# Attention and MLP on one core: input quarters made at other places of the unit and rounded by VectorE, first weights prepared over more units

## The chip, the cores and the metric

The kernel runs on one NeuronCore of a Trainium2 chip. The metric is the device time of one execution in microseconds (us). The engines are TensorE (PE; its weight loads are listed apart as PEld), VectorE (DVE), ScalarE (ACT), GpSimd (POOL) and the SyncE queue (SP), from which nearly all DMAs are issued.

## What is computed

Attention with a bias that is a small network of the relative position, then a two-layer network over the 2304 tokens. Cut to what matters:

```python
scores = scale * (q @ k.T) + bias          # bias[h, i, j] from a 32-unit network of log1p|i-j| / log1p(i)
attn = exp(scores - max) / (sum + 1e-9)    # 4 batches, 8 heads, 576 positions, head size 64
x = (attn @ v) reordered to (2304, 512)
h = x @ w_in                               # 512 -> 2048
g = where(h >= 1, h, where(h <= -1, 0, (h + 1)**2 / 4))
out = g @ w_out                            # 2048 -> 512
```

## The kernel before, in words

Every product is done with both operands split into a rounded high part (type fp32r) and a low part, the difference: three matmuls stand for one. A split therefore costs one rounding copy and one subtraction. The subtractions are mostly POOL's.

The program has three stages. The first makes the bias tables and stores them to DRAM. The second is attention: 16 units, one for each pair of heads and batch (unit n has heads pair p = n // 4 and batch b = n % 4). The third is the two-layer network, in three blocks of 768 tokens; for the first block its input x must be ready in 8 quarters (k, j): k is the pair of heads, j the half of 384 tokens.

The order of all work in attention is written out by hand. Each step of a unit has a time in the table `BEAT`, in a scale of 15.5 a unit; `on(n, t, f)` puts a step at 15.5 * n + t, and the steps are emitted in the order of these numbers. ACT, DVE, PE and POOL keep that order, so a time only sets what stands before what on an engine. On DVE one unit has, in this order (numbers modulo 15.5): `r` 0.47 (adds a constant to the row sums and inverts them; line 547, tile `sum`), maxima `m00` 1.38 and `m01`, the low parts `l30` and `lL`, maxima `m10` and `m11`, `ls1`, `kh` 6.08 (rounding of the next keys and queries, line 171), maxima `m20` and `m21`, `l10` 8.9, `vh` 9.52 (rounding of the values, line 179), `l11` 10.73, `m30` 11.36, `ls0`, `m31` 12.43, `mL` 13.97, `l21` 14.68. The maxima are line 457 and read the scores in PSUM; the low parts are line 544 and read PSUM too. POOL has in one unit: low part of the values (line 147, `vs`) 0.57, then a copy and a subtraction (lines 541 and 542) for each of four of the transposed tiles, `l31` 2.47, `l00` 8.55, `l01` 12.22, `l20` 14.3, and two subtractions for keys and queries (line 147, `ls`) at 8.73 and 10.32. PE holds two score tiles (`S`) at a time; a maximum frees one.

Between these steps stand two kinds of early work for the third stage. `split_x` makes one quarter: it loads two half sums of x from DRAM with the inverted row sums, and then `add` (line 391), `scaled` (line 394), `high` (line 398, the rounding, on ACT) and `rest` (line 402, POOL). `XQ` gives for each quarter the time of its load, the place in SBUF (`raw`, `x` or `bias`, three pools that have other users too) and the unit and times of the four steps. All four lie in one unit: (0,0) in unit 4, (1,0) in 8, (2,0) in 12, (0,1) in 13, (1,1) in 14, the last three in unit 15. `weight_ahead` prepares a tile of weights, rebuilt from two 32-bit halves of its 64-bit words: `load`, `shift` and `sign` on ACT, `join` and `high` on DVE (lines 127 and 132), `rest` on POOL (line 136). `WQ` puts the first four tiles in units 6, 7, 10 and 11, all five steps of a tile in one unit. A load that needs a buffer waits in SP's queue for the buffer's last reader, and what is behind it waits too.

Of the kernel before, what the change touches and what calls it, by code (L numbers as in the profile page):

```python
# [24 lines left out]
NG = S // 16  # L25
# [4 lines left out]

CBW = (1, 1, 32, C, C, C * H, S // 4, NG)
CB = sum(CBW)
CFG = dict(un=[('paaa', 'paav')[g in (1, 30, 32, 34)] for g in range(NG)], bb=5, mv=1, rb='a', pool=((0, 0), (0, 1), (2, 0), (3, 1)), sb=4, keep=1, drain=2, diag='a', rb2='v', eps='v', rc=2, rbb=1, hb=2, rawb=(2, 2), eb=4, seq=0, pb=(6, 9, 12, 14, 16), pq=22, tb=6, ub=12, low0='ppp', anch=(8, 8, 16, 23, 23), low1='ppp', ob=4, gb=4, fin=2, sbf=('v', 'v', 'v', 'v', 'v'), bsE=(), ytail='p')
EPS = 1e-9
RB = 2
FIRST = ((0, 3), (1, 5), (2, 33))
USUAL = (10.0, 13.1, 14.05, 17.9)
XQ = {(0, 0): (39, "raw", 4, USUAL), (1, 0): (80, "raw", 8, USUAL), (2, 0): (120, "raw", 12, USUAL), (3, 0): (140, "bias", 15, (6.1, 6.2, 8.0, 8.1)),
      (0, 1): (125, "x", 13, USUAL), (1, 1): (133, "raw", 14, USUAL), (2, 1): (144, "x", 15, (9.5, 10.0, 10.9, 11.1)), (3, 1): (153, "raw", 15, (13.1, 13.2, 14.5, 16.3))}
WQ = {(0, 0): (53, 6), (0, 1): (70, 7), (1, 0): (93, 10), (1, 1): (110, 11)}  # L40
LB = ((1, 1), (2, 1), (3, 2), (3, 3), (2, 3))
UNIT = 15.5
BEAT = {
# [11 lines left out]
}  # L55
POOL, SB, KEEP, RBB = CFG["pool"], CFG["sb"], CFG["keep"], CFG["rbb"]
BIG = 3.0e38
# [4 lines left out]
def attn_cpb_moe_kernel(ctx, tc, qk, vL, cb, win, wout, lw, ident, ii, out):  # L62
    nc = tc.nc
# [19 lines left out]
    lp = ctx.enter_context(tc.tile_pool(name="a_load", side="right", bufs=2))  # L83
    bp = loads.enter_context(tc.tile_pool(name="a_bias", side="right", bufs=CFG["bb"]))
    qp = loads.enter_context(tc.tile_pool(name="a_qkv", side="right", bufs=2))
# [54 lines left out]
    qkv, bias = {}, {}  # L140
# [8 lines left out]
    def keep(ins):  # L149
        tc.keep_in_program_order(ins)  # L150

    def pool(ins):
        if KEEP and go[0]:
            tc.keep_in_program_order(ins)
# [5 lines left out]
    def prep(n):  # L160

        L = CFG["low0"] if n == 0 else CFG["low1"] if n == 1 else "ppp"
        a = qkv[n] = {}

        def high(ins):
            keep(ins)

        def high_k():

            a["h"] = qp.tile([P, KQ], F32R, tag="kh", name=f"kh{n}", bufs=CFG["hb"])  # L170
            high(nc.vector.tensor_copy(a["h"], a["r"]))

        def load_r():
            a["r"] = lp.tile([P, KQ], F32, tag="qk", name=f"qk{n}", bufs=CFG["rawb"][0])
            nc.sync.dma_start(out=a["r"], in_=qk[n])
# [5 lines left out]
        def load_v():  # L181
            a["rv"] = lp.tile([P, 10, D], F32, tag="v", name=f"v{n}", bufs=CFG["rawb"][1])
            nc.sync.dma_start(out=a["rv"].rearrange("p a b -> p (a b)"), in_=vL[n])
# [20 lines left out]
    with ExitStack() as ph:  # L204
# [21 lines left out]
        diag = [ac.tile([P, P], F32, name=f"diag{i}") for i in range(2)]  # L226
# [9 lines left out]
        pq = cp.tile([P, 2, C, H], F32, name="pq")  # L236
# [102 lines left out]
    xs = {}  # L339
# [3 lines left out]
    def x_tile(z, k, part, name):  # L343
        if z == 0:
            return xp0.tile([P, TH], F32R, tag=f"x{'hl'[part]}{k}", name=name)
        at = 2 * k + part
        g = min(at // 3, 2) + (at == 7)
        if at % 3 == 0 or at == 7:
            tag, w, n_ = ("qk", KQ, CFG["rawb"][0]) if g < 2 else ("v", 10 * D, CFG["rawb"][1])
            room[g] = lp.tile([P, w], F32R, tag=tag, name=name, bufs=n_)  # L350
        c0 = TH * (at % 3 if at < 6 else 0)
        return room[g][:, c0 : c0 + TH]

    def load_x(blk, k, j, home="x"):

        src = xT[k][blk // TB][:, :, TH * j : TH * j + TH].rearrange("(s d) i c -> d s i c", s=2)
        rp = rps[0]
        if home != "raw":
            if home == "bias":
                r = bp.tile([P, 2 * S], F32, tag="bias", name=f"x{blk}_{k}_{j}").rearrange("p (a b) -> p a b", a=3)  # L360
            else:
                r = rp.tile([P, 3, TH], F32, tag="x", name=f"x{blk}_{k}_{j}", bufs=1)
            r, rr = r[:, 0:2], r[:, 2]
        else:
            r = rp.tile([P, 2 * DM], F32, tag="raw", name=f"x{blk}_{k}_{j}")[:, : 2 * TH].rearrange("p (a b) -> p a b", a=2)
            rr = rp.tile([P, DM], F32, tag="a", name=f"xr{blk}_{k}_{j}")[:, :TH]
        for i in range(2):
            nc.sync.dma_start(out=r[D * i : D * i + D], in_=src[:, :, i])
        c0 = blk + TH * j
        c1 = c0  # L370
        while c1 < c0 + TH:
            t = c1 % S
            e = min(c0 + TH, c1 - t + (512 if t < 512 else S))
            for i in range(2):
                at = 512 * i + t if t < 512 else 1024 + D * i + t - 512
                row = rT[k][c1 // S][at : at + e - c1].unsqueeze(0)
                nc.sync.dma_start(out=rr[D * i : D * i + D, c1 - c0 : e - c0], in_=row.to_broadcast((D, e - c1)))  # L377
            c1 = e
        return r, rr
# [5 lines left out]
    def split_x(k, j, home):  # L385

        r, rr = load_x(0, k, j, home)
        x = r[:, 0]

        def add():  # L390
            keep(nc.vector.tensor_tensor(out=x, in0=x, in1=r[:, 1], op=ALU.add))

        def scaled():
            keep(nc.vector.tensor_tensor(out=x, in0=x, in1=rr, op=ALU.mult))  # L394

        def high():
            xs[k, j] = [x_tile(j, k, i, f"x{'hl'[i]}0_{k}_{j}") for i in range(2)]
            keep(nc.scalar.copy(xs[k, j][0], x))

        def rest():  # L400
            h, l = xs[k, j]
            pool(nc.gpsimd.tensor_tensor(out=l, in0=x, in1=h.bitcast(F32), op=ALU.subtract))

        return add, scaled, high, rest

    with ExitStack() as ph:
        tp1 = ph.enter_context(tc.tile_pool(name="a_eT1", bufs=1))
# [35 lines left out]
        def on(n, t, f, *a):  # L443
            events.append((UNIT * n + t, len(events), f, a))
# [180 lines left out]
                on(B * (p - 1) + b, 3.1 * k_ + 0.5, load_b)  # L625

        def plan_x(k, j):
            T, home, n, ts = XQ[k, j]
            fs = []

            def load():
                assert all((k, t_) in made for t_ in range(TH * j, TH * j + TH))
                fs.extend(split_x(k, j, home))

            on(T // 10, T % 10 * UNIT / 10, load)
            for i, t in enumerate(ts):
                on(n, t, lambda i=i: fs[i]())

        for kj in XQ:
            plan_x(*kj)  # L640
        for fo, (T, n) in WQ.items():
            load, *fs = weight_ahead(*fo, rps[0])
            on(T // 10, T % 10 * UNIT / 10, load)
            for t, f in zip((6.85, 11.0, 13.1, 15.4, 17.9), fs):
                on(n, t, f)
        go[0] = True
        while events:
            i = min(range(len(events)), key=lambda i: events[i][:2])
            _, _, f, a = events.pop(i)
# [5 lines left out]
    with ExitStack() as ph:  # L655
# [204 lines left out]
        for f in range(2, NF):  # L860
            for o in range(2):
                m = 2 * f - 4 + 3 * o
# [13 lines left out]
        for k in range(2):  # L876
            t = T1 + 1 + 12 * k
# [17 lines left out]
        for blk in (0, TB):  # L895
            for m in range(2 * NF):
                f, j = m // 2, m % 2
# [50 lines left out]
        for g in range(NG2):  # L948
            blk, f = b2, 2 * g
            for s_ in range(NS):  # L950
                t = NS * g + s_
# [30 lines left out]
                else:  # L982
                    fo, j = {2: (f, 0), 4: (f + 1, 1), 5: (f + 1, 0), 6: (f, 1)}[s_]
# [80 lines left out]
```

## Time and profile before

| what | us |
|---|---|
| median of 3 runs | 738.35 (737.07 to 740.10) |
| the profiled execution, its own time | 736.86 |
| its span, first to last instruction | 734.5 |
| mean granted TensorE clock | 0.994 |
| PE busy of the span | 695.0 |
| DVE, ACT and POOL busy | 530.4, 512.4, 514.0 |

Times in the rows are us from the start of the span. Attention runs from about 68 to 333 us, the two-layer network from there to the end. An instruction's time runs from its start on the engine to its end, and holds whatever it stood still for after its start.

### The profile page before, as it was taken

The page shows a single profiled execution, that of the slowest core. Times are in us where ns is not written, and L with a number is a line of the kernel's source. Part 1 is how long each engine was busy: PE and PEld are TensorE (multiplying, and loading weights), DVE is VectorE, ACT ScalarE, POOL GpSimd, SP SyncE. Part 2 cuts the span into 40 slices and gives each one's busy share as a digit, 9 for nine tenths or more (in the row PEclk, how much of TensorE's full clock was granted, in tenths as well). Part 3 has the DMA queues.
Part 4 walks back from the last instruction along what each step waited for, and adds up shares of the span by engine and source line. Part 5 has one row for each costly group of instructions (what it writes and reads, how often), then busy time and mean ns, then how long its engine had stood idle before and what let it go on. Part 6 is the DMA issues. An engine that isn't in the chain of part 4 may idle for free.

```text
span 734.5 us, 14012 instructions
## 1 busy us (share of the span) xinstructions
PE 695.0 (95%) x4864; PEld 600.4 (82%) x4864; DVE 530.4 (72%) x1009; ACT 512.4 (70%) x1124; POOL 514.0 (70%) x444
## 2 busy tenths in 40 slices
PE   5677999999999999989999999999999999999997
PEld 2234899889989988779988989999999888888886
DVE  7999887989897899986767776454555565666653
ACT  8996889889989988884655646344444457666563
POOL 7985788877978997774675868566656555666652
PEclk9999999999999999999999999999999999999999
DMA  6789335535752653344446462222021001000002
GB/s 194 230 254 295 119 119 182 174 116 148 234 166 87 198 173 109 92 118 152 146 147 197 144 194 91 87 64 65 1 65 33 1 16 72 1 2 1 0 1 86
DMA packets 51237, 83.97 MB, mean 114 GB/s; under 512 B 11216, under 2 KB 31456, under 8 KB 51168
## 3 DMA queue, kind: packets, MB, share of 16 engines
q1 hardware_dynamic: 50880, 82.87, 36.2%
q8 instruction: 38, 0.62, 0.4%
q14 instruction: 31, 0.25, 0.1%
q10 hardware_dynamic: 288, 0.22, 0.1%
HBM read 57.95 MB, written 25.12 MB: 113 GB/s over the span
## 4 chain that ended last, share of the span: by engine, by line
PE 60%; DVE 11%; POOL 6%; ACT 5%; issue 4%; DMA 3%; SPq 2%; DVEq 0%; POOLq 0%; ACTq 0%
PE y L672 21%; PE h L672 13%; PE p L672 7%; PE O L431 6%; PE S L431 5%; PE T L434 4%; DVE e L457 3%; POOL lo L542 2%; DMA x<-rT 1%; DVE x L394 1%; DVE lo L544 1%; SPq L377 1%; DVE sum L547 1%; PE T_s L434 1%; PE S_L L431 1%
## 5 line engine op out<-in xcount | busy, mean ns | idle before, releaser
L914 POOL TENSOR_TENSOR gl<-c,gh 128x384 fp32r<-128x384 f32 x64 | 70.6, 1104 | 101.9 <-issue 86.9
L672 PE MATMUL y<-w1h,gl 128*128 128x512 f32 x288 | 113.8, 395 | 0.0
L672 PE MATMUL y<-w1l,gh 128*128 128x512 f32 x288 | 113.5, 394 | 0.0
L672 PE MATMUL y<-w1h,gh 128*128 128x512 f32 x288 | 112.0, 389 | 0.0
L454 ACT ACTIVATE e<-e,mx 128x576 f32<-128x576 f32 x128 | 99.1, 775 | 18.4 <-DVE mx L457 17.2
L457 DVE CUSTOM_DVE_ANT_0 e<-S,bias 128x576 f32<-128x576 f32 x128 | 92.0, 747 | 13.9 <-PE S L431 13.9
L542 POOL TENSOR_TENSOR lo<-c,hi 128x512 fp32r<-128x512 f32 x64 | 85.2, 1331 | 5.1
L732 ACT ACTIVATE c<-c,half_s 128x384 f32<-128x384 f32 x64 | 39.4, 616 | 62.4 <-DVE c L729 62.3
L434 PE MATMUL T<-id_s,e 128*128 128x128 f32 x512 | 73.5, 277 | 1.7 <-DVE lo L544 1.6
L541 POOL CAST hi<-c 128x512 fp32r<-128x512 f32 x64 | 44.1, 689 | 43.0 <-ACT c L533 42.9
L938 POOL TENSOR_TENSOR gl<-c,gh 128x384 fp32r<-128x384 f32 x32 | 32.7, 1022 | 47.8 <-issue 22.3
L434 PEld LDWEIGHTS T<-id_s,e 128*128 128x128 f32 x512 | 59.5, 143 | 6.5 <-ACT e L454 2.8
L672 PEld LDWEIGHTS y<-w1h,gl 128*128 128x128 f32 x288 | 54.0, 187 | 11.5
L672 PEld LDWEIGHTS y<-w1l,gh 128*128 128x128 f32 x288 | 54.0, 188 | 7.8
L672 PEld LDWEIGHTS y<-w1h,gh 128*128 128x128 f32 x288 | 54.1, 188 | 7.6
L270 ACT ACTIVATE u<-lw,nthr 128x576 f16<-128x576 f32 (+17 forms) x104 | 57.5, 644 | 3.9 <-DVE lw L235 2.4
L289 PEld LDWEIGHTS <-qh 128*32 128x32 f16 x704 | 19.0, 101 | 47.8 <-issue 20.6
L431 PE MATMUL O<-hi,vs 128*128 128x256 f32 (+1 forms) x320 | 57.0, 308 | 0.3 <-ACT x L569 0.3
L272 POOL TENSOR_SCALAR u<-lw,thr 128x576 f16<-128x576 f32 (+17 forms) x36 | 51.7, 1451 | 7.2 <-DVE lw L235 4.0
L431 PE MATMUL S<-kh 64*128 64x288 f32 x256 | 49.4, 346 | 6.5 <-DVE mx L457 5.6
L431 PE MATMUL O<-lo,vs 128*128 128x256 f32 (+1 forms) x320 | 55.3, 303 | 0.0
L729 DVE TENSOR_SCALAR c<-h 128x384 f32<-128x384 f32 x64 | 35.4, 552 | 27.2 <-PE h L672 25.4
(263 smaller groups left out, 2052.5 us busy)
## 6 DMA issues: line engine op xcount, KB each, us to landing
bias_d<-y SPq DMA_DIRECT2D x36, 295.5 KB
qk<-in_qk_dram SPq DMA_DIRECT2D x16, 640.0 KB
x<-xT SPq DMA_DIRECT2D x48, 192.0 KB
raw<-in_win_dram SPq DMA_DIRECT2D x16, 512.0 KB
raw<-in_wout_dram SPq DMA_DIRECT2D x16, 512.0 KB
v<-in_vL_dram SPq DMA_DIRECT2D x16, 320.0 KB
bias<-bias_d SPq DMA_DIRECT2D x16, 288.0 KB
out_dram<-o SPq DMA_DIRECT2D x17, 256.0 KB
```

The costliest lines, as they stand in the source:

```text
L270: tc.keep_in_program_order(nc.scalar.activation(u[:, :n_], lw1[:, :n_], AF.Sigmoid, bias=nthr[:, m : m + 1], scale=STEEP))
L272: EN[x].tensor_scalar(out=u[:, :n_], in0=lw1[:, :n_], scalar1=thr[:, m : m + 1], scalar2=None, op0=ALU.is_gt)
L431: keep(nc.tensor.matmul(*a, **k))
L434: keep(nc.tensor.transpose(*a))
L454: keep(nc.scalar.activation(ev, ev, AF.Exp, bias=m, scale=-1.0, accum_out=sm[:, at : at + 1]))
L457: keep(nc.vector.tensor_tensor_reduce(out=o.rearrange("p (a b) -> p a b", a=2), in0=ps[:, :, :HS], in1=of.rearrange("p (a b) -> p a b", a= ...
L541: keep(nc.gpsimd.tensor_copy(hi, ps))
L542: keep(nc.gpsimd.tensor_tensor(out=lo, in0=ps, in1=hi.bitcast(F32), op=ALU.subtract))
L672: a = nc.tensor.matmul(out, w, x, start=start, stop=stop)
L729: keep(nc.vector.tensor_scalar(out=c, in0=h, scalar1=-1.0, scalar2=1.0, op0=ALU.max, op1=ALU.min))
L732: keep(nc.scalar.activation(c, c, AF.Square, scale=0.5, bias=half_s))
L914: keep(nc.gpsimd.tensor_tensor(out=gl, in0=c, in1=gh.bitcast(F32), op=ALU.subtract))
```

## The change

Three edits. (1) The list `XQ` gives each step of a quarter a unit of its own. `high` is no longer a step: the rounding follows `scaled` at once and is a `tensor_copy` of VectorE where it was a copy of ScalarE. A quarter now has its `add` late in one unit (15.4, between `l21` and `r`), `scaled` with the rounding in the next (13.1, between `m31` and `mL`) and `rest` at 20.0 of that, which is 4.5 of the unit after (on POOL behind `l31`). The three quarters of unit 15 have times of their own. (2) Four quarters instead of one live in the bias pool, which gets seven buffers for five. (3) The list `WQ` starts the four weight tiles in units 1, 3, 5 and 7, and spreads the steps of each over three units: `shift` at 11.1; a unit later `sign` at 11.1 and `join` at 13.1; another unit later `high` at 9.96 (between `vh` and `l11`) and `rest` at 20.0.

So VectorE has: unit 2, 4 and 6 a `join`; 3, 5 and 7 a weight's `high`; 8 a `join` and an `add`; 9 a weight's `high`, `scaled` with rounding, and an `add`; 10, 13 and 14 `scaled` with rounding and an `add`; 11 `scaled` with rounding; 12 an `add`.

```diff
-CFG = dict(... bb=5, ...)
+CFG = dict(... bb=7, ...)
...
-USUAL = (10.0, 13.1, 14.05, 17.9)
-XQ = {(0, 0): (39, "raw", 4, USUAL), (1, 0): (80, "raw", 8, USUAL), (2, 0): (120, "raw", 12, USUAL), (3, 0): (140, "bias", 15, (6.1, 6.2, 8.0, 8.1)),
-      (0, 1): (125, "x", 13, USUAL), (1, 1): (133, "raw", 14, USUAL), (2, 1): (144, "x", 15, (9.5, 10.0, 10.9, 11.1)), (3, 1): (153, "raw", 15, (13.1, 13.2, 14.5, 16.3))}
-WQ = {(0, 0): (53, 6), (0, 1): (70, 7), (1, 0): (93, 10), (1, 1): (110, 11)}
+XQ = {(0, 0): (70, "bias", (8, 15.4), (9, 13.1), (9, 20.0)), (1, 0): (81, "bias", (9, 15.4), (10, 13.1), (10, 20.0)),
+      (2, 0): (102, "raw", (10, 15.4), (11, 13.1), (11, 20.0)), (0, 1): (125, "raw", (12, 15.4), (13, 13.1), (13, 20.0)),
+      (1, 1): (120, "x", (13, 15.4), (14, 13.1), (14, 20.0)), (3, 0): (140, "bias", (14, 15.4), (15, 6.1), (15, 7.0)),
+      (2, 1): (145, "raw", (15, 9.5), (15, 13.1), (15, 15.0)), (3, 1): (147, "bias", (15, 15.4), (15, 16.0), (15, 17.9))}
+WQ = {(0, 0): (10, 1), (0, 1): (30, 3), (1, 0): (50, 5), (1, 1): (70, 7)}
...
         def scaled():
             keep(nc.vector.tensor_tensor(out=x, in0=x, in1=rr, op=ALU.mult))
-
-        def high():
             xs[k, j] = [x_tile(j, k, i, f"x{'hl'[i]}0_{k}_{j}") for i in range(2)]
-            keep(nc.scalar.copy(xs[k, j][0], x))
+            keep(nc.vector.tensor_copy(xs[k, j][0], x))
...
-        return add, scaled, high, rest
+        return add, scaled, rest
...
-            T, home, n, ts = XQ[k, j]
+            T, home, *ts = XQ[k, j]
...
-            for i, t in enumerate(ts):
+            for i, (n, t) in enumerate(ts):
                 on(n, t, lambda i=i: fs[i]())
...
-            for t, f in zip((6.85, 11.0, 13.1, 15.4, 17.9), fs):
-                on(n, t, f)
+            for m, t, f in zip((0, 1, 1, 2, 2), (11.1, 11.1, 13.1, 9.96, 20.0), fs):
+                on(n + m, t, f)
```

## Rows read from the trace of the kernel before

**Rows 1.** Busy time by engine in a clean unit and in the network.

```profile
core 0: us, PE busy (x) PEld busy (x) DVE busy (x) ACT busy (x) POOL busy (x), PEclk, DMA share, GB/s
98.50:113.90 15.40, 15.40 (x140) 14.03 (x139) 13.09 (x30) 14.01 (x38) 12.20 (x12) 1.00 0.41 121
345.00:420.00 75.00, 74.52 (x375) 67.20 (x375) 56.82 (x86) 44.15 (x78) 51.60 (x41) 1.00 0.51 159
```

**Rows 2.** Timeline, VectorE: `kh` in units 2, 4, 5, 6, 14.

```profile
104.27 0.82 DVE L171 CAST kh<-qk 128x1280 fp32r<-128x1280 f32 x1
...
134.99 0.82 DVE L171 CAST kh<-qk 128x1280 fp32r<-128x1280 f32 x1
...
152.61 0.81 DVE L171 CAST kh<-qk 128x1280 fp32r<-128x1280 f32 x1
...
167.82 0.82 DVE L171 CAST kh<-qk 128x1280 fp32r<-128x1280 f32 x1
...
298.14 0.82 DVE L171 CAST kh<-qk 128x1280 fp32r<-128x1280 f32 x1
```

**Rows 3.** Timeline, VectorE in unit 4, which makes a quarter.

```profile
138.91 1.91 DVE L391 TENSOR_TENSOR x<-x 128x384 f32<-128x384 f32 x1
...
142.35 0.74 DVE L457 CUSTOM_DVE_ANT_0 e<-S,bias 128x576 f32<-128x576 f32 x1
...
143.02 1.56 DVE L394 TENSOR_TENSOR x<-x,xr 128x384 f32<-128x384 f32 x1
...
145.64 0.69 DVE L544 TENSOR_TENSOR lo<-T,hi 128x512 fp32r<-128x512 f32 x1 [0.39 <-ACT hi L536]
146.41 1.57 DVE L547 TENSOR_SCALAR sum<-sum 128x9 f32<-128x9 f32 x1
...
148.14 0.70 DVE L457 CUSTOM_DVE_ANT_0 e<-S,bias 128x576 f32<-128x576 f32 x1
```

**Rows 4.** Timeline, GpSimd in unit 4.

```profile
138.59 3.64 POOL L147 TENSOR_TENSOR ls<-qk,kh 128x640 fp32r<-128x640 f32 x2
...
142.87 1.29 POOL L542 TENSOR_TENSOR lo<-c,hi 128x512 fp32r<-128x512 f32 x1
144.11 0.95 POOL L541 CAST hi<-c 128x512 fp32r<-128x512 f32 x1
...
146.38 1.57 POOL L147 TENSOR_TENSOR vs<-v,vs 128x640 fp32r<-128x640 f32 x1
```

**Rows 5.** Timeline, TensorE at the first scores that wait in unit 4.

```profile
148.90 0.40 PE L431 MATMUL S<-kh 64*128 64x288 f32 x1 [0.61 <-DVE mx L457]
```

**Rows 6.** Timeline, VectorE in unit 2, which has no early work.

```profile
110.03 0.75 DVE L457 CUSTOM_DVE_ANT_0 e<-S,bias 128x576 f32<-128x576 f32 x1
...
112.96 0.69 DVE L544 TENSOR_TENSOR lo<-T,hi 128x512 fp32r<-128x512 f32 x1 [0.26 <-ACT hi L536]
...
114.97 0.76 DVE L457 CUSTOM_DVE_ANT_0 e<-S,bias 128x576 f32<-128x576 f32 x1 [0.82 <-PE S L431]
```

**Rows 7.** Timeline, GpSimd in unit 2.

```profile
107.87 3.34 POOL L147 TENSOR_TENSOR ls<-qk,kh 128x640 fp32r<-128x640 f32 x2
...
113.09 0.62 POOL L541 CAST hi<-c 128x512 fp32r<-128x512 f32 x1
```

**Rows 8.** Timeline, VectorE: `m00` behind unit 6, which prepares weights.

```profile
178.77 0.70 DVE L457 CUSTOM_DVE_ANT_0 e<-S,bias 128x576 f32<-128x576 f32 x1
```

**Rows 9.** Timeline, VectorE in unit 15.

```profile
319.38 0.86 DVE L391 TENSOR_TENSOR x<-x 128x384 f32<-128x384 f32 x1
320.28 0.85 DVE L394 TENSOR_TENSOR x<-x 128x384 f32<-128x384 f32 x1
...
327.39 0.25 DVE L547 TENSOR_SCALAR sum<-sum 128x9 f32<-128x9 f32 x1 [0.33 <-ACT e_L L454]
```

**Rows 10.** Timeline, GpSimd in unit 15.

```profile
319.76 0.95 POOL L541 CAST hi<-c 128x512 fp32r<-128x512 f32 x1
...
327.56 1.02 POOL L402 TENSOR_TENSOR xl<-x,xh 128x384 fp32r<-128x384 f32 x1
```

**Rows 11.** Timeline, TensorE near the end of attention.

```profile
326.51 0.44 PE L672 MATMUL h<-xh,w0h 128*128 128x384 f32 x1 [0.94 <-DVE mx L457]
```

More of the change, by code (lines that the diff above doesn't have):

```diff
@@ L32 @@
 CB = sum(CBW)
-CFG = dict(un=[('paaa', 'paav')[g in (1, 30, 32, 34)] for g in range(NG)], bb=5, mv=1, rb='a', pool=((0, 0), (0, 1), (2, 0), (3, 1)), sb=4, keep=1, drain=2, diag='a', rb2='v', eps='v', rc=2, rbb=1, hb=2, rawb=(2, 2), eb=4, seq=0, pb=(6, 9, 12, 14, 16), pq=22, tb=6, ub=12, low0='ppp', anch=(8, 8, 16, 23, 23), low1='ppp', ob=4, gb=4, fin=2, sbf=('v', 'v', 'v', 'v', 'v'), bsE=(), ytail='p')
+CFG = dict(un=[('paaa', 'paav')[g in (1, 30, 32, 34)] for g in range(NG)], bb=7, mv=1, rb='a', pool=((0, 0), (0, 1), (2, 0), (3, 1)), sb=4, keep=1, drain=2, diag='a', rb2='v', eps='v', rc=2, rbb=1, hb=2, rawb=(2, 2), eb=4, seq=0, pb=(6, 9, 12, 14, 16), pq=22, tb=6, ub=12, low0='ppp', anch=(8, 8, 16, 23, 23), low1='ppp', ob=4, gb=4, fin=2, sbf=('v', 'v', 'v', 'v', 'v'), bsE=(), ytail='p')
 EPS = 1e-9
```

## The prediction

> **What bounds the kernel now.** I read the busy times by stretch first. In a unit without early work TensorE is busy for all of 15.40 us, and in the two-layer network for 74.52 of 75.00 [rows 1]. So TensorE is the bound wherever nothing holds it up, the network behind attention neither gives nor takes anything, and a microsecond won or lost in a unit arrives whole at the end.
>
> Then I used the rounding of the keys, `kh`, which comes once a unit, as a clock of the units [rows 2]. From unit 2 to unit 4 it advances 30.72 us, two clean units of 15.36. From unit 4, which makes a quarter, to unit 5 it advances 17.62, which is 2.26 too many. From unit 2 to unit 14 it advances 193.87 against 12 * 15.36 = 184.32: the four units 4, 8, 12 and 13 cost 9.55 together, 2.39 each. With unit 14, whose cost comes after its `kh`, the five units cost 11.95 us. That is all the change can win there. Unit 6 rebuilds weights with the same engines; the `m00` behind it starts 10.95 after its `kh`, in the clean unit 10.70 [rows 2, 6, 8]. It costs next to nothing.
>
> Third, the timeline of VectorE and GpSimd in unit 4 [rows 3, 4], to see where the 2.26 arise. The work of `add` is small; its 1.91 us are waiting. GpSimd's two `ls` take 3.64 around it, in the clean unit 3.34 [rows 4, 7]. `scaled` starts at 143.02, GpSimd's `lo` ends at 144.16, `scaled` ends at 144.58: a turn of 0.42. GpSimd's `hi`, begun at 144.11, ends at 145.06, 0.48 behind that. `sum` on 128x9 elements takes 1.57, ending with GpSimd's `vs`. So VectorE's work on SBUF alone and GpSimd's work take turns. In unit 15 `add` and `scaled` follow one another and GpSimd's `hi` (0.95 for a usual 0.62) still comes between [rows 7, 9, 10]: whoever waits is next. The Trainium skill says the same of the port that the two share (page "SBUF — State Buffer", section "Who interferes with whom"), and counts copies and casts from SBUF to SBUF on VectorE among the instructions that need it. By that the rounding on ScalarE needed no turn and on VectorE needs one, which speaks against that edit.
>
> The price to TensorE is read at `m00` of the next unit, which frees a tile of scores. In unit 4 it starts 13.15 after `kh`, 2.45 later than in unit 2; TensorE waits there, 0.61 in one row [rows 5], and the unit is 2.26 longer. The rule for what follows: `m00` may be 0.2 late for nothing, and then each 0.1 costs 0.1.
>
> **The change part by part.** All times are us after `kh` of the unit, replayed from [rows 6, 7]. In the clean unit `m31` ends at 6.51, `ls` at 6.94, `l21` at 9.38, the `hi` beside it at 9.44, and `m00` starts at 10.70.
>
> *Removed:* 11.95 us in units 4, 8, 12, 13 and 14. ScalarE loses eight copies; it was not what the scores waited for, so that is worth nothing by itself, except that `l21` waited 0.39 for ScalarE in unit 4 [rows 3] and 0.26 without a quarter, which is in the replay.
>
> *Scaled with rounding at 13.1 and `add` at 15.4 (units 10, 13, 14).* `scaled` waits for `ls` until 6.94 and runs to 7.36; GpSimd's `hi` 0.48, to 7.84; the rounding, which no row shows at this size. By elements it is 384/1280 of the 0.82 of `kh`, 0.25; the other bound is those 0.82; I take 0.3, to 8.14. `mL`, 0.75, ends before 8.9, and `l21` ends at about 9.45, little changed. GpSimd's `lo` (I take 1.2 of its 1.29, since a waiting instruction has its start behind it) and next `hi` end at about 9.9; `add` 0.42, 10.3; GpSimd's `lo` 1.2, 11.5; `sum` and the inverse 0.25. `m00` is at 11.75 with whole turns and at 11.6 where starts overlap, 0.9 to 1.05 late: 0.7 to 0.85, taken as 0.8. Unit 8, with a `join` for `scaled` and no rounding, ends in the same turns: 0.8. Four units, 3.2. Lower bound 0.3 each (GpSimd a little later, so that VectorE gets two turns in a row), upper 2.4, as unit 4.
>
> *`scaled` alone (unit 11):* `sum` waits for `hi` to 9.9 and `m00` stays at 10.70: nothing. Without the 0.8 of idle time before `m00` [rows 6] it would cost 0.5.
>
> *`add` alone (unit 12):* it waits for `hi` to 9.44, runs to 9.86, `lo` to 11.06, `sum` and inverse to 11.3: 0.6 late, 0.4. If `lo` starts first, 1.8.
>
> *A weight's `high` at 9.96 (units 3, 5, 7).* This is the place of `add` in unit 4, between `vh` and `l11`, and GpSimd's `ls` run there. In unit 4 `m31` starts 7.36 after `kh`, in unit 2 5.76: 1.6 late on VectorE [rows 2, 3, 6]. TensorE takes back most of that in the pause before `mL`; the rest is what remains of the 2.26 when the 1.7 of the later part are taken off: 0.5 each, 1.5 for three. Bounds 0 and 0.9. Before, this copy stood at 15.4 and belonged to the units that cost nothing.
>
> *Unit 9 has all three.* As in unit 4 to 144.58; then `hi` to 145.06, rounding 145.36, `mL` 146.1, `l21` 146.8. GpSimd's `lo` ends at 146.5 and its `vs` (1.57) starts before `add` is ready, to 148.1; `add` to 148.5, GpSimd's next `hi` to 149.0, `sum` and inverse to 149.2. That is 3.5 late for the clean unit: 3.3. Bounds 1.9 (VectorE wins the turn from `vs`) and 3.6.
>
> *Moved at no cost:* `rest` at 4.5 falls in a stretch where GpSimd has no step between `l31` and `l00`; it can delay `kh` by a part of 1.02 [rows 10], and VectorE has over 0.8 idle in the unit. `shift` at 11.1 takes the place of `sign`. Queue and buffers: the load of (2,0) at 3.1 of unit 10 waits for the last `rest` of a weight, some 4 us, with a bias load, a row sum and a key load behind it that are read a unit or more later. With seven buffers each bias tile is loaded where its last reader is a unit back or more, as before. The weights' loads are early. I cost all this at 0, and at 2 if SP's wait were to reach the keys.
>
> *Unit 15.* Before, `add` and `scaled` of the last quarter stand ahead of `mL`, and TensorE waits 0.94 [rows 11]. After, `scaled` and rounding of (2,1) stand there: some 0.5 to 1.0 sooner. But the rounding of (3,1) now comes after `sum`: from 327.39 it ends at about 328.8 with the inverse, `scaled` and the rounding, and the `rest` that started at 327.56 [rows 9, 10] starts there, ahead of `l31` on GpSimd, which TensorE's last products need: 1.25 later. Bounds -1.0 and +1.3; I take +0.6, since matmuls of the network can fill part of it.
>
> *Sum:* 3.2 + 0.4 + 1.5 + 3.3 = 8.4 for 11.95, so 3.55 won, less 0.6 in unit 15: 2.95. The profiled execution's own time is 736.86, so 733.9; it lies 1.49 under the median of 738.35, so the median should come to 735.4.
>
> **Rivals.** A measurement of this kernel tells about 0.5% (3.7 us) from no change.
>
> *The places are free.* Taken apart, no step costs TensorE anything, as unit 6 speaks for. Against: its copy and its `join` had the idle 0.8 to themselves, and no unit showed `high` ahead of `l11`. Then 11.95 less the 0.6 of unit 15: 727.0.
>
> *Given back.* As forecast, but GpSimd's turns fall badly in two of the four double units (2.4 for 0.8): 3.2 more, 738.6. The change then does nothing measurable.
>
> *Slower.* In all four double units `l21` ends after GpSimd's `lo` has started (it is 0.4 too late for that). Then `add` waits for `lo` and `sum` for `vs`, 1.57 more, as in [rows 3, 4]. The price is 3.1 each as in unit 9: 4 * 2.3 = 9.2 more, 744.6. ScalarE's `hi` before `l21` is what decides; it has lost a copy, which speaks against.
>
> **How the numbers follow.** The forecast with its bounds (733 to 738) has 0.60, free places 0.10, given back 0.18, slower 0.12. Won are 2.95 us in the middle of the forecast, so it passes 3.7 us in somewhat under half of its cases: 0.27, with the free places 0.37 faster; 0.12 slower; the other 0.51 the same. The range 730.5 to 740 leaves out the free places and the larger part of the slower case.
>
> **What would show it.** The step from `kh` to `kh`: 15.9 in units 3, 5 and 7, 16.2 in 10 and 13, 15.8 in 12, 18 to 19 in 9, 15.4 in 11. `add` at 15.4 with 0.6 to 0.9 us, not 1.9; `sum` over 1 us in units 8, 10, 13 and 14. The roundings with 0.5 to 0.9. Wrong would be: units at 15.4 throughout, or `sum` at 1.5 and `add` at 1.5 in every double unit, or an attention stage held by a load.

## The result, and the profile after

The changed kernel takes 730.77 us (median of 4 runs, 729.90 to 732.55), the kernel before 738.19 in the same job (4 runs, 737.07 to 740.10): ratio 0.990, 95% interval 0.987 to 0.993. It is 7.4 us faster; 735.4 was forecast, inside a range of 730.5 to 740.

Where the time came from is read from TensorE's timeline: the first matmul of the last scores (`S_L`) of unit 0 and of unit 15, in the kernel before and in the changed one.

```profile
80.11 0.40 PE L431 MATMUL S_L<-kh 128*128 128x288 f32 x1 [0.97 <-DVE mx L457]
...
322.45 0.40 PE L431 MATMUL S_L<-kh 128*128 128x288 f32 x1
```

```profile
81.06 0.40 PE L430 MATMUL S_L<-kh 128*128 128x288 f32 x1 [0.79 <-DVE mx L456]
...
317.54 0.38 PE L430 MATMUL S_L<-kh 128*128 128x288 f32 x1
```

Attention between these points takes 236.48 for 242.34: 5.86 won. From there to the first matmul of the second product (`y`) it is 15.86 for 16.84, another 0.98 won. Against that the profiled execution of the changed kernel is 0.95 later at the first point and its network is 0.66 longer, so that the spans differ by 5.2 only (729.3 for 734.5). Two things go with the late start, and how much each makes of it was not tried. The busy times by stretch show a lower granted clock in the changed kernel (the column behind POOL; kernel before, then the changed one):

```profile
0.00:68.00 68.00, 45.43 (x706) 19.13 (x708) 61.67 (x129) 60.25 (x107) 56.84 (x47) 0.97 0.76 238
68.00:83.00 15.00, 12.66 (x98) 10.44 (x98) 10.87 (x25) 10.32 (x24) 7.82 (x8) 0.89 0.69 216
```

```profile
0.00:68.00 68.00, 45.91 (x704) 19.03 (x704) 61.32 (x128) 60.23 (x107) 56.86 (x47) 0.95 0.77 245
68.00:83.00 15.00, 12.76 (x89) 10.34 (x90) 10.48 (x25) 9.37 (x23) 6.96 (x7) 0.77 0.72 212
```

From 68 to 83 us all traces of this document have 0.77 or 0.78 but that of the kernel before. In experiment 7, with 0.77, the first `S_L` still starts at 80.10, so the clock is not all of it. The change probably has a part, though no step before unit 1 was moved: in the three traces with five bias buffers (the kernel before, experiments 4 and 7) the DMAs move 238 to 240 GB/s in the first 68 us and the first scores start at 67.38 to 67.88; in the ten with seven buffers it is 244 to 246 GB/s, and nine of them start at 68.15 to 68.43 (one at 67.67). Experiment 8, which has nothing of the change but the buffers, is one of the nine.

Unit by unit, from the `S_L` of one unit to that of the next (worked out from TensorE's timeline as above). A unit in which TensorE loses nothing takes 15.35 to 15.39.

| from unit | before | after | VectorE's early steps after it, in the changed kernel |
|---|---|---|---|
| 2, 4, 6 | 15.35, 17.02, 15.35 | 15.68, 15.68, 15.70 | `high` of units 3, 5, 7 |
| 3, 5, 7 | 15.93, 15.37, 16.24 | 15.39, 15.37, 15.38 | none but `join` in 4, 6 and 8, beyond it |
| 8 | 16.99 | 15.70 | `add` in 8, `high` in 9 |
| 9 | 15.37 | 17.88 | rounding and `add` of unit 9 |
| 10, 13, 14 | 15.35, 17.61, 17.15 | 16.00, 15.97, 15.99 | rounding and `add` |
| 11 | 16.24 | 15.37 | rounding alone |
| 12 | 17.62 | 15.61 | `add` alone |

The timelines of VectorE and of GpSimd in unit 10 of the changed kernel, the answer to [rows 3, 4]:

```profile
238.50 0.94 DVE L395 TENSOR_TENSOR x<-x 128x384 f32<-128x384 f32 x1
239.47 0.65 DVE L397 CAST xh<-x 128x384 fp32r<-128x384 f32 x1
240.04 0.75 DVE L456 CUSTOM_DVE_ANT_0 e_L<-S_L,biasL 128x576 f32<-128x576 f32 x1
...
240.72 0.68 DVE L543 TENSOR_TENSOR lo<-T,hi 128x512 fp32r<-128x512 f32 x1
241.32 0.92 DVE L392 TENSOR_TENSOR x<-x 128x384 f32<-128x384 f32 x1
242.17 1.25 DVE L546 TENSOR_SCALAR sum<-sum 128x9 f32<-128x9 f32 x1
...
243.58 0.70 DVE L456 CUSTOM_DVE_ANT_0 e<-S,bias 128x576 f32<-128x576 f32 x1
```

```profile
238.95 0.95 POOL L540 CAST hi<-c 128x512 fp32r<-128x512 f32 x1
239.98 1.29 POOL L541 TENSOR_TENSOR lo<-c,hi 128x512 fp32r<-128x512 f32 x1
241.22 0.61 POOL L540 CAST hi<-c 128x512 fp32r<-128x512 f32 x1
241.91 1.47 POOL L541 TENSOR_TENSOR lo<-c,hi 128x512 fp32r<-128x512 f32 x1
```

The turns are those of the replay: `scaled`, `hi`, rounding, `lo`, `hi`, `add`, `lo`, `sum`. `add` waits for the second `hi` (241.22 to 241.83) and not for a `lo`; `sum` waits for one `lo`, 1.25, and not for `vs`. `m00` starts 11.52 after its `kh` (232.06): 0.82 later than in the clean unit, 0.9 to 1.05 were forecast.

### The profile page after: what moved, and what is told of

The parts are those of the page before. It is cut to its first block, busy times and chain, and to the rows that moved or that the text cites. A ratio compares the mean times of both kernels' runs of the same rounds, so it can differ in the third digit from the quotient of the medians.

```text
span 729.3 us, 13989 instructions
## 1 busy us (share of the span) xinstructions
PE 695.0 (95%) x4864; PEld 600.7 (82%) x4864; DVE 529.8 (73%) x1017; ACT 509.2 (70%) x1116; POOL 510.9 (70%) x444
## 4 chain that ended last, share of the span: by engine, by line
PE 65%; DVE 10%; ACT 6%; DMA 5%; issue 2%; SPq 2%; POOL 1%; ACTq 0%; DVEq 0%; POOLq 0%
PE y L671 22%; PE h L671 14%; PE O L430 8%; PE p L671 7%; PE S L430 6%; PE T L433 5%; DVE e L456 2%; DVE lo L543 2%; ACT e L453 2%; PE S_L L430 1%; DMA xT<-x 1%; PE T_s L433 1%; DMA x<-xT 1%; DMA x<-rT 1%; PE T_L L433 1%
## 5 line engine op out<-in xcount | busy, mean ns | idle before, releaser
L541 POOL TENSOR_TENSOR lo<-c,hi 128x512 fp32r<-128x512 f32 x64 | 83.4, 1303 | 5.1
L734 DVE TENSOR_TENSOR c<-h,c 128x384 f32<-128x384 f32 x64 | 35.5, 554 | 26.4 <-ACT c L731 25.6
```

Source lines behind the costliest of these rows:

```text
L541: keep(nc.gpsimd.tensor_tensor(out=lo, in0=ps, in1=hi.bitcast(F32), op=ALU.subtract))
L734: keep(nc.vector.tensor_tensor(out=c, in0=h, in1=c, op=ALU.max))
```

## The experiments

Two theories stood against one another at first. *Turns:* what an early step costs is what VectorE waits for GpSimd (and the reverse) around it, and that is set by its place. *ScalarE:* the gain is that eight copies left ScalarE. Others came up on the way. Ratios are to the kernel before, run beside each. The numbers are those by which the expectations name one another; where the text goes by another order, it follows the argument.

**Experiment 1: Rounding back on ScalarE.** The changed kernel with one line of it undone.

```diff
-            keep(nc.vector.tensor_copy(xs[k, j][0], x))
+            keep(nc.scalar.copy(xs[k, j][0], x))
```

> The changed kernel with the rounding of the quarters back on ScalarE (behind scaled), all else as changed. Turns (a step costs what VectorE waits for GpSimd between its other steps): the rounding has one turn on VectorE behind scaled, and the add behind it waits for the same GpSimd step with or without it, so m00 moves by 0.1 at most; ScalarE's copy stands ahead of the copy that l21 waits for, as in the kernel before, so l21 and all behind it come later and add may miss its turn: 0 to 3 us more than the changed kernel, 731 to 734. ScalarE relieved (the rival: the gain is that eight copies left ScalarE): most of the 7.4 us is lost, 736 to 738.

739.63 us, ratio 1.002 (1.000 to 1.004): the whole gain is gone, and more than either theory expected. The trace tells how. VectorE's and GpSimd's timeline in unit 10:

```profile
240.86 0.69 DVE L543 TENSOR_TENSOR lo<-T,hi 128x512 fp32r<-128x512 f32 x1 [1.15 <-ACT hi L535]
241.47 1.43 DVE L392 TENSOR_TENSOR x<-x 128x384 f32<-128x384 f32 x1
242.81 1.53 DVE L546 TENSOR_SCALAR sum<-sum 128x9 f32<-128x9 f32 x1
```

```profile
241.19 1.29 POOL L541 TENSOR_TENSOR lo<-c,hi 128x512 fp32r<-128x512 f32 x1
242.43 1.89 POOL L148 TENSOR_TENSOR vs<-v,vs 128x640 fp32r<-128x640 f32 x1
```

```profile
238.74 0.52 ACT L397 CAST xh<-x 128x384 fp32r<-128x384 f32 x1 [0.36 <-DVE x L395]
...
240.24 0.59 ACT L535 CAST hi<-T 128x512 fp32r<-128x512 f32 x1
```

ScalarE's rounding stands ahead of its copy `hi` (the rows above), so `l21` waits 1.15 for `hi`; `add` comes 0.28 after GpSimd's `lo` has started, waits it out, and `sum` meets `vs`. This is the slower rival of the prediction in units 10 and 13 (17.66 and 19.24 from `S_L` to `S_L`), not in unit 8 (15.70), which has no rounding. The profiled execution, with 737.37 one of the shorter ones, has 242.09 of attention for the changed kernel's 236.48. It leaves open whether the copy's length or its place does it.

**Experiment 5: Rounding on ScalarE, behind `hi`.** The same as a step of its own at 14.9.

```diff
+        def high():
+            xs[k, j] = [...]
+            keep(nc.scalar.copy(xs[k, j][0], x))
...
-XQ = {(0, 0): (70, "bias", (8, 15.4), (9, 13.1), (9, 20.0)), ...
+XQ = {(0, 0): (70, "bias", (8, 15.4), (9, 13.1), (9, 14.9), (9, 20.0)), ...
```

> The changed kernel with the rounding of the quarters on ScalarE, as in the first experiment, but as a step of its own at 14.9, behind ScalarE's copy hi (14.08) for which l21 waits (in unit 15 at the changed kernel's places). Lost race (what the first experiment seems to show: a copy in front of hi makes l21 late, add starts after GpSimd's lo and sum after its vs): l21 and add are back in their turns, units 10, 13 and 14 cost 0.6 each again, 730 to 733. ScalarE relieved (rival: the eight copies of 0.51 on ScalarE are what costs, wherever they stand): 736 to 740 as in the first experiment.

730.48 us, ratio 0.991 (0.989 to 0.993), the changed kernel's time. ScalarE has its eight copies back, and only their place differs from experiment 1. Units 10, 13 and 14 take 16.22, 15.99 and 15.98; unit 9 takes 18.91, 1.0 more than in the changed kernel. In unit 10 `hi` is first on ScalarE, and `l21` starts as soon as it is done:

```profile
240.94 0.59 ACT L537 CAST hi<-T 128x512 fp32r<-128x512 f32 x1
241.42 0.52 ACT L399 CAST xh<-x 128x384 fp32r<-128x384 f32 x1
```

```profile
241.56 0.69 DVE L545 TENSOR_TENSOR lo<-T,hi 128x512 fp32r<-128x512 f32 x1
```

So the amount of ScalarE's work is not what counts; that nothing stands in front of `hi` is.

**Experiment 4: The kernel before, rounding on VectorE.** One line of the change alone, at its old place 14.05.

```diff
-            keep(nc.scalar.copy(xs[k, j][0], x))
+            keep(nc.vector.tensor_copy(xs[k, j][0], x))
```

> The kernel before with one edit, the rounding of the quarters on VectorE, at its own place 14.05 between mL and l21. Turns: the rounding waits for GpSimd's copy there and l21 follows later, against ScalarE's copy that no longer stands before l21's own: within 2 us of the kernel before, 737 to 740. ScalarE relieved (rival): 731 to 734.

741.41 us, ratio 1.005 (1.003 to 1.006): 3.7 us slower than the kernel before beside it, so the ScalarE theory is out here too; the loss is over what the turns were expected to cost (within 2 us). In unit 4 the rounding takes its turn right behind a `lo` that has just started:

```profile
145.97 1.46 DVE L398 CAST xh<-x 128x384 fp32r<-128x384 f32 x1
```

That costs unit 4 next to nothing, 17.10 for 17.02, since `sum` then takes 0.91 for 1.57. The trace has the loss later: 0.96 in unit 14 (18.11 for 17.15), and 2.06 between the `S_L` of unit 15 and the first `y` (18.90 for 16.84). There the same turn makes `l21` late, and TensorE waits for it; in the kernel before it waited 0.46 at this place, for ScalarE:

```profile
328.26 1.44 DVE L398 CAST xh<-x 128x384 fp32r<-128x384 f32 x1
329.62 0.68 DVE L544 TENSOR_TENSOR lo<-T,hi 128x512 fp32r<-128x512 f32 x1
```

```profile
330.45 0.97 PE L434 MATMUL T_L<-id_s,e_L 128*128 128x128 f32 x4 [1.60 <-DVE lo L544]
```

**Experiment 2: The quarters in one unit again.** The changed kernel, with the steps of the first five quarters at 10.0, 13.1 and 17.9 of units 4, 8, 12, 13 and 14, and the weights spread as in the change.

```diff
-XQ = {(0, 0): (70, "bias", (8, 15.4), (9, 13.1), (9, 20.0)), ...
+XQ = {(0, 0): (39, "bias", (4, 10.0), (4, 13.1), (4, 17.9)), ...
```

> The changed kernel with the first five quarters made in one unit each again (units 4, 8, 12, 13, 14; add 10.0, scaled with the rounding 13.1, rest 17.9); the weights stay spread over three units. Turns: the five units cost 2.2 to 2.9 each again, 12 to 14 us, for the 4.3 that units 8 to 14 cost now beyond the weights, and high at 9.96 keeps its 0.33 four times: 738 to 741, no better than the kernel before. Weights (the rival: the gain comes from weights and loads that start early): it stays at 731 to 733.

743.19 us, ratio 1.007 (1.005 to 1.009), above the 738 to 741 expected of the turns. The early weights by themselves win nothing; their rival is out. Part of the loss is that units 4 and 8 now hold a `join` as well: from their `S_L` 18.94 and 19.71, while units 12 and 13, which hold a quarter alone, take 17.62 and 17.63, as before the change.

**Experiment 8: Seven buffers alone.** The kernel before with `bb=7` and the quarters (0,0) and (1,0) in the bias pool.

> The kernel before with seven bias buffers and the quarters (0,0) and (1,0) in them, all steps at their old places. Turns: buffers and loads were no part of the wait: 737 to 739, as before. Buffers (rival): 733 or less.

737.27 us, ratio 1.000 (0.999 to 1.002). By themselves the buffers win nothing. That the change needs them, so that a quarter can wait for its next step without holding up other loads, was not tried.

**Experiment 7: `vs` later.** The kernel before, no early step moved; GpSimd's subtraction for the values goes from 0.57 to 5.0.

```diff
-    "vl": 0.57,
+    "vl": 5.0,
```

> The kernel before, no early step moved, but GpSimd's subtraction for the values (vs, 1.56) from 0.57 to 5.0 of its unit, behind l31, into the stretch in which GpSimd waits. Turns: sum, which ended with vs in every unit that made a quarter, finds GpSimd free; m00 comes some 1.4 earlier there and the five units cost about 1.0 instead of 2.4 each, less what kh now waits: 6 us faster than before, 731 to 733. If sum's 1.57 were its own or VectorE's work (rival): 737 to 739.

736.60 us, ratio 0.9995 (0.998 to 1.001): a miss in time. `sum` does find `vs` gone, but GpSimd's next step, the `rest` of the quarter, takes the turn: `sum` takes 1.01 for 1.57, and unit 4 16.45 for 17.02.

```profile
146.42 1.01 DVE L547 TENSOR_SCALAR sum<-sum 128x9 f32<-128x9 f32 x1
```

```profile
146.39 1.01 POOL L402 TENSOR_TENSOR xl<-x,xh 128x384 fp32r<-128x384 f32 x1
```

And `vs` is now late for others: the units behind the last weights' `rest`, 7 and 11, go from 16.24 to 17.53 and 17.57, with one wait of TensorE for 1.7 in each.

**Experiment 3: `high` back at 15.4.** The changed kernel; `high` of the weights stands in the unit of the `join` again.

```diff
-            for m, t, f in zip((0, 1, 1, 2, 2), (11.1, 11.1, 13.1, 9.96, 20.0), fs):
+            for m, t, f in zip((0, 1, 1, 1, 2), (11.1, 11.1, 13.1, 15.4, 20.0), fs):
```

> The changed kernel with the weights' high back at 15.4 of the unit that has the join (units 2, 4, 6, 8), where it cost nothing before. Turns: units 3, 5 and 7 lose 0.32 each, unit 9 falls from 2.51 to the 0.63 of units 10, 13 and 14, unit 8 with join, high and add goes from 0 to 0.6 or so: 2.2 us faster than the changed kernel, 728 to 729. If high at 9.96 is not what costs there (rival): 731, and unit 9 stays at 17.9.

728.67 us, ratio 0.987 (0.986 to 0.989), 2.1 less than the changed kernel. Against the kernel before beside each it is 1.6 more won, and the two intervals overlap; what shows the effect is the trace. The steps from units 2, 4 and 6 fall from 15.68 to 15.35, that from unit 9 from 17.88 to 16.01; unit 8 pays 0.63 for having three steps. Attention is 2.2 shorter. `high` at 9.96 is the part of the change that costs more than what it replaced.

**Experiment 6: `add` behind `kh`.** On top of experiment 3: `add` goes from 15.4 to 6.1 of the unit that has `scaled`.

```diff
-XQ = {(0, 0): (70, "bias", (8, 15.4), (9, 13.1), (9, 20.0)), ...
+XQ = {(0, 0): (70, "bias", (9, 6.1), (9, 13.1), (9, 20.0)), ...
```

> The third experiment (high at 15.4 of the join's unit) with add moved from 15.4 to 6.1 of the unit that has scaled, right behind kh, where GpSimd has no step. Turns: add takes 0.55 there in VectorE's idle time, sum no longer waits behind it; units 8 to 14 lose nearly all of the 3.8 that they still cost in the third experiment: 725 to 726. Amount of work (rival: it is the number of early steps in a unit that costs, not their place): 728 to 729 as the third.

727.81 us, ratio 0.988 (0.986 to 0.991): between the two expectations, and by ratio no better than experiment 3, so the times do not tell place from amount. The trace does: attention from `S_L` to `S_L` is 232.84 for 234.30 in experiment 3 and 236.48 in the changed kernel. Thirteen of the 15 steps take 15.35 to 15.39. Units 9 and 10 take 16.13 and 17.00, since GpSimd has two `rest` in unit 10, and `add` waits there:

```profile
226.74 1.01 POOL L401 TENSOR_TENSOR xl<-x,xh 128x384 fp32r<-128x384 f32 x1
227.71 1.86 POOL L137 TENSOR_TENSOR w1l<-a,w1h 128x512 fp32r<-128x512 f32 x1
```

```profile
228.36 1.64 DVE L392 TENSOR_TENSOR x<-x 128x384 f32<-128x384 f32 x1
```

**Experiment 9: All weights' `rest` a unit earlier**, on top of experiment 6, to take the second `rest` out of unit 10.

```diff
-            for m, t, f in zip((0, 1, 1, 1, 2), (11.1, 11.1, 13.1, 15.4, 20.0), fs):
+            for m, t, f in zip((0, 1, 1, 1, 1), (11.1, 11.1, 13.1, 15.4, 20.0), fs):
```

> The sixth experiment with the weights' rest a unit earlier (20.0 of the join's unit), so that no unit has two of GpSimd's rests behind l31; in the sixth, unit 10 had two, kh and add waited for them, and units 9 and 10 cost 2.4. Turns: all 15 steps from unit to unit at 15.35 to 15.4, 2.4 less than the sixth: attention 230.6 us from unit 0 to unit 15, the kernel 724.5 to 726. If something else of unit 10 costs (rival, the load of (2,0) that stands in the queue there): units 9 and 10 stay at 16.1 and 17.0, 727 to 728.

726.82 us, ratio 0.984 (0.983 to 0.986), 0.8 over the range expected. Units 9 and 10 are at 15.37 and 15.35 as expected, but units 2, 4, 6 and 8 go from 15.35 to 15.95, 15.86, 15.85 and 15.83, so attention is 232.51, hardly less. Unit 2, whose own work and that ahead of it are the same in both kernels, shows how; VectorE and then GpSimd, first with `rest` later, then with `rest` earlier:

```profile
114.10 0.42 DVE L133 CAST w0h<-a 128x512 fp32r<-128x512 f32 x1
114.43 0.58 DVE L546 TENSOR_SCALAR sum<-sum 128x9 f32<-128x9 f32 x1
```

```profile
114.11 0.87 POOL L540 CAST hi<-c 128x512 fp32r<-128x512 f32 x1
```

```profile
114.36 0.88 DVE L133 CAST w0h<-a 128x512 fp32r<-128x512 f32 x1
115.17 1.26 DVE L546 TENSOR_SCALAR sum<-sum 128x9 f32<-128x9 f32 x1
```

```profile
114.35 0.61 POOL L540 CAST hi<-c 128x512 fp32r<-128x512 f32 x1
115.04 1.35 POOL L541 TENSOR_TENSOR lo<-c,hi 128x512 fp32r<-128x512 f32 x1
```

In the one, `high` starts 0.01 ahead of GpSimd's `hi` and takes 0.42; in the other 0.01 behind it and takes 0.88, and `sum` then meets the next `lo`. Two hundredths decide 0.6 us of the unit.

**Experiment 10: Only the last weight's `rest` earlier**, to tell the race from the `rest`.

```diff
-            for m, t, f in zip((0, 1, 1, 1, 2), (11.1, 11.1, 13.1, 15.4, 20.0), fs):
+            for m, t, f in zip((0, 1, 1, 1, 2 - (fo == (1, 1))), (11.1, 11.1, 13.1, 15.4, 20.0), fs):
```

> The sixth experiment with only the last weight's rest a unit earlier, so that unit 10 has one rest as all others. The ninth took away the 2.4 of units 9 and 10, but units 2, 4, 6 and 8 went from 15.36 to 15.9 each; the trace shows high and GpSimd's hi starting within 0.03 us of one another there, and GpSimd first. Race (high at 15.4 is a matter of hundredths): 230.6 us from unit 0 to unit 15 where VectorE is first in these units, up to 232.6 where it is not; the kernel 724.5 to 727. Rest (rival: the earlier rest itself costs the 0.5): 15.36 in the three units whose rest is not moved, 15.85 for the one that is, 231.1.

729.20 us, ratio 0.989 (0.987 to 0.990), over the 724.5 to 727 expected; attention, 232.50, is inside what was expected of it. The units from 2, 4 and 6, whose `rest` is where it was, take 15.95, 15.85 and 15.85 where experiment 6, with the same steps up to there, took 15.35: the race, not the `rest`. One execution of each was traced, so how often either side wins is not known.

**Experiment 11: The first three `high` behind `kh`**, where there is nothing to race with.

```diff
+            last = fo == (1, 1)
-            for m, t, f in zip((0, 1, 1, 1, 2 - (fo == (1, 1))), (11.1, 11.1, 13.1, 15.4, 20.0), fs):
+            for m, t, f in zip((0, 1, 1, 2 - last, 2 - last), (11.1, 11.1, 13.1, 15.4 if last else 6.1, 20.0), fs):
```

> The tenth with high of the first three weights not at 15.4 but at 6.1 of the next unit, behind kh, where add stands in other units and GpSimd has no step to race with. Race: units 2 to 7 at 15.35 to 15.39 without a toss, 230.6 to 231.1 from unit 0 to unit 15, the kernel 724.5 to 726. Rival (the rest costs, or high costs wherever it stands): units 3, 5 and 7 at 15.6 or more, no better than the tenth.

728.50 us, ratio 0.989 (0.987 to 0.990), a miss in time (724.5 to 726 were expected). Units 2 to 7 take 15.35 to 15.37, as expected of the race. But units 8 and 9 take 15.81 and 17.01, so attention is 232.54 again: in unit 9 the last weight's `rest` (212.01, 1.29) and `kh` meet, `kh` waits to 1.65, and `add` behind it comes late.

```profile
212.01 1.29 POOL L137 TENSOR_TENSOR w1l<-a,w1h 128x512 fp32r<-128x512 f32 x1
```

```profile
212.34 1.65 DVE L172 CAST kh<-qk 128x1280 fp32r<-128x1280 f32 x1
```

The four last versions have attention stages of 232.5 to 232.8, 3.6 to 4.0 shorter than the changed kernel's. Yet against the kernel before beside each they win only 9.7, 11.0, 8.0 and 8.7 for its 7.4, 0.6 to 3.6 more. In the profiled executions of the last three the network, from the first `y` to the end, is longer (397.1 to 399.4 for 395.9): in experiment 10 TensorE waits 3.2 in its first block for a VectorE step, in the changed kernel 1.0.

```profile
PE h L671 <- DVE c L734: 3.2, 5, 1.0
```

Ahead of some of these late steps VectorE stands in its order for a half of a weight from ScalarE (2.35 and 2.41; 0.99 at most in that stretch of experiment 6) or for a load (3.02 and 2.60, which other traces have too). What makes ScalarE late there was not tried and stays open. The version with all weights' `rest` a unit earlier has the best ratio to the kernel before, 0.984 against 0.990 for the change; the intervals of these two do not meet.

## Why the prediction was right, point by point

**The whole.** The mechanism held, the size did not: 7.4 us were won where 2.95 was forecast, and the time lies 0.3 inside the lower end of the range, which owes that to its width. No measurable change, given 0.51, did not come; a gain beyond 3.7 us, given 0.37, did. Two terms of the sum were off: the new places cost 2.5 less than forecast, and unit 15 was 1.6 better.

**The bound and what could be won.** Held for the units: the five cost 11.95 by `kh`, and the clean units after are at 15.37. That the network gives and takes nothing holds between these two kernels to 0.66; over all traces it takes 394.3 to 399.4, so what is won in attention need not arrive whole.

**Turns.** Held, shown by the replay of unit 10, and by experiments that moved steps without changing their amount (attention changed by 2.2 us with the place of `high`, by 1.5 with that of `add`, by 4.4 with that of ScalarE's copy). The rule of the Trainium skill named in the prediction (page "SBUF — State Buffer", section "Who interferes with whom"), by which one engine holds the shared port for a whole instruction and the other waits, agrees with these rows; which of two waiters is next is read from the rows alone. That a rounding on VectorE needs a turn shows in unit 10 as 0.65 for what takes 0.36 where GpSimd is idle (unit 15, below; the replay took 0.3). The turn spoke against that edit, but it did not make the kernel slower than one with the copy on ScalarE (730.77 and, in experiment 5, 730.48).

**The sum.** 8.4 us was forecast for the new places, 5.93 was measured (236.48 less 15 times 15.37):

| term | forecast | measured |
|---|---|---|
| units 10, 13, 14 (rounding and `add`) | 0.8 each | 0.63, 0.60, 0.62 |
| unit 8 (`join` and `add`) | 0.8 | 0.0 |
| unit 9 (all three) | 3.3 | 2.84 |
| units 3, 5, 7 (`high` at 9.96) | 0.5 each | 0.31 to 0.32 |
| unit 12 (`add` alone) | 0.4 | 0.24 |
| unit 11 (`scaled` with rounding) | 0.0 | 0.0 |

None was sized too low; the largest miss is unit 8. There GpSimd is later by the `join`'s turn than I had it, `add` gets in ahead of `hi`, and `sum` is next:

```profile
207.72 0.62 DVE L392 TENSOR_TENSOR x<-x 128x384 f32<-128x384 f32 x1
208.27 0.57 DVE L546 TENSOR_SCALAR sum<-sum 128x9 f32<-128x9 f32 x1
```

```profile
207.87 0.94 POOL L540 CAST hi<-c 128x512 fp32r<-128x512 f32 x1
```

This is the case for which the prediction gave its lower bound (GpSimd a little later), and unit 8 came out below that bound of 0.3; `sum` over 1 us in unit 8, one of its signs, did not come. Unit 9 lies between its bounds: `add` loses to `vs` by 0.08, as replayed, and waits 1.88.

```profile
225.04 1.88 DVE L392 TENSOR_TENSOR x<-x 128x384 f32<-128x384 f32 x1
```

```profile
224.96 1.55 POOL L148 TENSOR_TENSOR vs<-v,vs 128x640 fp32r<-128x640 f32 x1
```

**Unit 15.** Wrong in sign: +0.6 forecast, -0.98 measured. I took from the kernel before that `sum` and what follows would stay where they were, and that the last `rest` would start at 328.8. In the changed kernel everything behind `mL` is earlier by what `mL` gained (1.1), GpSimd is idle there, so nothing waits for a turn, and the last `rest` starts 5.30 after `S_L`, 0.19 later than before and not 1.25:

```profile
321.41 0.16 DVE L546 TENSOR_SCALAR sum<-sum 128x9 f32<-128x9 f32 x1
...
321.81 0.56 DVE L395 TENSOR_TENSOR x<-x 128x384 f32<-128x384 f32 x1
322.41 0.36 DVE L397 CAST xh<-x 128x384 fp32r<-128x384 f32 x1
```

```profile
322.84 1.00 POOL L401 TENSOR_TENSOR xl<-x,xh 128x384 fp32r<-128x384 f32 x1 [2.02 <-DVE xh L397]
```

Together the two stretches give 5.86 + 0.98 = 6.8 where 3.55 - 0.6 = 2.95 was forecast; the medians differ by 7.4.

**ScalarE's copies "worth nothing by itself".** Half wrong. Their number is worth nothing (experiment 5), their place 4.4 us of attention and 9.2 of the median between experiments 1 and 5: with the copy in front of `hi` the slower rival comes true in two units. I weighed that rival at 0.12 because the copy had left ScalarE; experiment 1 shows that this was what kept it away. The change without VectorE's rounding (experiment 1, 739.63) and the kernel before with it (experiment 4, 741.41) are both slower than the kernel before. What wins are the spread steps with nothing in front of `hi`; the rounding on VectorE is one way to that, a later place on ScalarE (experiment 5, 730.48) another. The spread quarters with the weights at their old places were not run. In the working of that rival, 3.1 is called the price "as in unit 9", which has 3.3 in the sum; no chance hangs on it.

**Queues and buffers at nothing.** Held in attention: no wait of TensorE on a transfer appears there, and seven buffers alone leave the time as it was (experiment 8). Their earlier transfers may be part of the late start seen in the traces.

## What to carry to other kernels

Where two engines take turns, an early step costs what it waits for, and what its lateness makes the next step wait for; so replay the order of turns from the trace and put the step where the other engine has none, rather than count its work. A copy on a third engine can decide such a race by standing in front of what the next step needs: keep it behind. Before trusting a place, look how far the two starts are apart; a place that is won by hundredths of a microsecond is lost again by the next edit.

## What the runs showed of the hardware that was not expected

The same instruction of VectorE on 128x9 elements takes from 0.16 us, where GpSimd is idle, to 1.57, where it ends with a GpSimd instruction. A start 0.01 us earlier or later decides who has the next turn (0.42 or 0.88 us for the same copy). And the same early stage, between 68 and 83 us, ran at a mean granted clock of 0.89 in one traced execution and of 0.77 or 0.78 in the twelve others: from the first scores to the first `S_L` it takes 12.23 in the former and 12.47 to 13.19 in the latter. Spans of single executions of this kernel can't be compared to better than about 1 us.
